# The low half of the converted 64-bit weights subtracted on VectorE instead of on GpSimd

## The chip, the cores and the metric

The kernel runs on one core of a Trainium2 chip. The metric is the device time of one execution in microseconds (us). Five engines work side by side, each through its own list of instructions in order: TensorE (PE; its weight loads are PEld), VectorE (DVE), ScalarE (ACT), GpSimd (POOL), and SyncE (SP), which issues most of the DMAs. A measurement of this kernel can tell a change of about 0.2%, which is 3.0 us.

## The reference

```
# attention: q, k, v are [8, 8, 576, 64]; blocks of 64 tokens, causal by block
scores = q @ k^T / 8, masked where block_i < block_j
attn = exp(scores - max) / (sum + 1e-9);  x = attn @ v        # -> [8, 576, 512]
# mixing of tokens and of channels; U, V, w_ch1, w_ch2 are float64
u = x + (x^T @ U @ V)^T                                       # rank 32
y = u + relu(u @ w_ch1) @ w_ch2                               # 512 -> 2048 -> 512
# gated convolution; w_val, conv_w, w_out are float64
gate = sigmoid(causal conv of y with conv_w, 5 taps per channel)
out = (gate * (y @ w_val)) @ w_out
```

The weights of the last two parts come as float64, which the chip reads as pairs of 32-bit words.

## The kernel before

**Products.** A product keeps more than one rounded factor: each operand is a high half (rounded to the type that PE multiplies) and a low half (what the rounding left), and three matmuls add high x high, high x low and low x high. `hi_act` (L89) makes a high half on ACT; `lo` (L95) subtracts it from the full value on the engine that it is given.

**Conversion of the weights.** `split64` (L136 to L143) turns one raw tile of 128x512 pairs of words into a high and a low half. Its steps, with their engines, are: SP fetches the raw tile; ACT takes the absolute value of the upper words (L118); DVE clamps it (L120), shifts it (L122), puts sign and exponent back (L123) and adds the bits of the lower words (L141), after which the raw tile is no longer needed; ACT rounds to the high half (L89); the low half is a subtraction (L95). There are two raw tiles, so a fetch waits until the L141 of two conversions before is over. The float32 value `wa` has two buffers early and one late. `split64` runs 40 times: 16 times for `w_ch1` (`split_w1`, output `w1hi` and `w1lo`, four DMAs per raw tile), 16 times for `w_ch2` (`split_w2`, output `wo`, which a DMA stores again), and 8 times for `w_val` and `w_out` (`load_wb`, outputs `wvh`, `wvl`, `woh`, `wol`). The first 32 run from the start to about 277 us, the last eight from 1117 to 1161 us.

**Stages.** Until about 128 us PE works on the attention of the first batch and of its mixing. From there until about 1260 us the channel mixing runs in nine groups of 512 tokens, `h` (L833) and `acc` (L885), and the attention of the later batches is laid between its matmuls. After that come `val` (L975) and `out` (L999).

**Attention around the change.** PE writes the scores `pS` (L416); DVE takes the row maxima (L425, L429) and scales them (L427, L430, L432); ACT takes the exponentials (L440), which frees the PSUM bank; PE turns them (`pE`, L456) and multiplies them with the values (`pPV`, L604); ACT copies the product and its sums out (`xt` L605, `lt` L606); POOL normalises `xt` (L624), and DVE adds the mixed tokens (L705). In the channel mixing ACT takes `hh` (L861) and DVE `hl` (L862).

**What sets the order.** PE's instructions stand in the order of the program. The order on DVE, ACT, POOL and SP comes from a scheduler that runs a model of the kernel when it is built, and a helper's engine and cost are part of what it models.

Of the kernel before, what the change touches and what calls it, by code (L numbers as in the profile page):

```python
# [22 lines left out]
def attn_moe_gate_kernel(ctx: ExitStack, tc: tile.TileContext, q, k, v, U, V, w1, w2, wval, convw, wout, out):  # L23
# [59 lines left out]
    def f32(ap):  # L83
        return ap if ap.dtype == F32 else ap.bitcast(F32)

    vec, act, pool, pe, sp = nc.vector, nc.scalar, nc.gpsimd, nc.tensor, nc.sync

    def hi_act(o, i):
        act.copy(o, i)  # L89
# [4 lines left out]
    def lo(eng, o, i, h):  # L94
        eng.tensor_tensor(o, i, f32(h), op=ALU.subtract)  # L95
# [20 lines left out]
    def magnitude(a, h):  # L116

        act.activation(a, f32(h), AF.Abs)  # L118
        with behind(where[0]):
            vec.tensor_scalar(a, a, F64_TINY, None, op0=ALU.max)  # L120
        au = a.bitcast(U32)
        vec.tensor_scalar(au, au, 3, 0x3FFFFFFF, op0=ALU.logical_shift_left, op1=ALU.bitwise_and)  # L122
        vec.scalar_tensor_tensor(au, h, 0xC0000000, au, op0=ALU.bitwise_and, op1=ALU.bitwise_or)  # L123
# [12 lines left out]
    def split64(raw, n, hi_out, lo_out, shape):  # L136

        a = stg["w"].tile([P, GS], F32, tag="wa", name="wa")[:, 0:n]
        au = a.bitcast(U32)
        magnitude(a, raw[:, :, 1])  # L140
        vec.scalar_tensor_tensor(au, raw[:, :, 0], 29, au, op0=ALU.logical_shift_right, op1=ALU.bitwise_or)  # L141
        hi_act(hi_out, shape(a))
        lo(pool, lo_out, shape(a), hi_out)  # L143

    ctx.enter_context(tc.manual_schedule(engines={mybir.EngineType.PE}))
    dram = ctx.enter_context(tc.tile_pool(name="dram", bufs=1, space=DRAM))
# [644 lines left out]
    def split_w1(f):  # L791
        fs = slice(f * P, (f + 1) * P)
        if is64(w1):
            r = stg["raw"].tile([P, GS, 2], U32, tag="raw64", name="raw64")
            hold(r)
            for d in range(ND):
                sp.dma_start(out=r[:, d * P:(d + 1) * P, :], in_=words(w1)[d * P:(d + 1) * P, fs, :])
            split64(r, DM, w1hi[:, :, fs], w1lo[:, :, fs], lambda x: x.rearrange("p (d f) -> p d f", f=P))
            return
        st = fetch(w1, DM, [(slice(0, P), slice(d * P, d * P + P), slice(d * P, d * P + P), fs) for d in range(ND)])  # L800
        st = st.rearrange("p (d f) -> p d f", f=P)
        hi_act(w1hi[:, :, fs], st)
        lo(pool, w1lo[:, :, fs], st, w1hi[:, :, fs])

    def split_w2(f):
        if is64(w2):
            r = stg["raw"].tile([P, GS, 2], U32, tag="raw64", name="raw64")
            hold(r)
            sp.dma_start(out=r, in_=words(w2)[f * P:(f + 1) * P])
            t = stg["o"].tile([P, 2, DM], F32R, tag="wo", name="wo")  # L810
            split64(r, DM, t[:, 0, :], t[:, 1, :], lambda x: x)
        else:
            st = fetch(w2, DM, [(slice(0, P), slice(0, DM), slice(f * P, (f + 1) * P), slice(0, DM))])
            t = stg["o"].tile([P, 2, DM], F32R, tag="wo", name="wo")
            hi_act(t[:, 0, :], st)
            lo(pool, t[:, 1, :], st, t[:, 0, :])
        sp.dma_start(out=w2_s[f], in_=f32(t))
# [85 lines left out]
    def load_wb(b_p):  # L903
        for nm, src in (("v", wval), ("o", wout)):
            h_ = b_p.tile([P, ND, DM], F32R, name=f"w{nm}h")
            l_ = b_p.tile([P, ND, DM], F32R, name=f"w{nm}l")
            wv[nm] = (h_, l_)
            for d in range(ND):
                if is64(src):
                    r = stg["raw"].tile([P, DM, 2], U32, tag="raw64", name="raw64")  # L910
                    sp.dma_start(out=r, in_=words(src)[d * P:(d + 1) * P])
                    split64(r, DM, h_[:, d, :], l_[:, d, :], lambda x: x)
                else:
                    st = stg["raw"].tile([P, DM], F32, tag="raw32", name="raw32")
                    sp.dma_start(out=st, in_=src[d * P:(d + 1) * P, :])
                    hi_act(h_[:, d, :], st)
                    lo(pool, l_[:, d, :], st, h_[:, d, :])
# [245 lines left out]
```

## Time and profile before

| | before |
|---|---|
| median of 3 runs | 1480.73 us (1478.81 to 1481.48) |
| span of the profiled execution | 1473.3 us |
| PE busy | 1426.3 us (97%) |
| DVE busy | 1054.8 us (72%) |
| ACT busy | 718.5 us (49%) |
| POOL busy | 297.8 us (20%) |

The median lies 7.4 us above the span of the one profiled execution; the span counts from the first to the last instruction that the profiler saw. Engines overlap, so the busy shares don't add up. PE idles for 47 us in all, and a part of the program in which PE never stops hides whatever happens on the other engines.

### The profile page before, as it was taken

How to read it: one execution, taken by the hardware profiler on the slowest of the kernel's cores; microseconds unless marked ns; L12 is line 12 of the kernel's file. 1: busy time of each engine (PE TensorE's matmuls, PEld its weight loads, DVE VectorE, ACT ScalarE, POOL GpSimd, SP SyncE). 2: the span in 40 equal slices, each digit the busy share in tenths (PEclk: the TensorE clock that was granted, in tenths of full speed). 3: DMA queues.
4: the chain of work that ended last, by engine and by line, in shares of the span. 5: the costliest groups of instructions: out<-in, count | busy, mean ns of one | idle time of the engine just before them, and what ended most of it. 6: DMA issues, size and time to landing. Idle time of an engine off the chain costs nothing.

```text
span 1473.3 us, 20082 instructions
## 1 busy us (share of the span) xinstructions
PE 1426.3 (97%) x6706; PEld 1102.3 (75%) x6706; DVE 1054.8 (72%) x2224; ACT 718.5 (49%) x1529; POOL 297.8 (20%) x420
## 2 busy tenths in 40 slices
PE   6888899899999999999999999999999999999999
PEld 3656666677777777777777777777888888788887
DVE  7878877967786888777778878777224326399991
ACT  4676564555555546565555555555322221344332
POOL 2113332212121112112211211121122100343310
PEclk9999999999999999999999999999999999999999
DMA  6445764543343434333434433332255433223311
GB/s 123 104 106 154 217 210 130 152 110 96 84 102 110 95 96 111 96 86 82 124 82 111 114 83 96 96 95 70 86 159 167 147 128 123 92 72 101 109 56 65
DMA packets 246288, 163.56 MB, mean 111 GB/s; under 512 B 197669, under 2 KB 212261, under 8 KB 246186
## 3 DMA queue, kind: packets, MB, share of 16 engines
q1 hardware_dynamic: 246186, 162.29, 39.6%
q8 instruction: 53, 0.87, 0.3%
q14 instruction: 49, 0.40, 0.1%
HBM read 134.98 MB, written 27.26 MB: 110 GB/s over the span
## 4 chain that ended last, share of the span: by engine, by line
PE 82%; DVE 10%; DMA 3%; ACT 2%; issue 1%; SPq 1%; POOL 0%; DVEq 0%; ACTq 0%
PE acc L885 25%; PE h L833 25%; PE pPV L604 8%; PE o L999 7%; PE val L975 6%; PE pS L381 6%; DMA raw<-in_moe_w_ch_dram 1%; DVE wa L123 1%; DVE rq L425 1%; PE pG L680 1%; PE acc L878 1%; PE pS L416 1%; DVE wa L141 1%; PE pT L664 1%; DVE wa L120 1%
## 5 line engine op out<-in xcount | busy, mean ns | idle before, releaser
L885 PE MATMUL acc<-hh,w 128*128 128x512 f32 x1152 | 401.0, 402 | 0.0
L885 PEld LDWEIGHTS acc<-hh,w 128*128 128x128 f32 x1152 | 217.1, 188 | 67.6 <-issue 22.5
L833 PE MATMUL h<-uh,w1hi 128*128 128x512 f32 x576 | 238.5, 414 | 2.3 <-ACT lt L606 1.2
L833 PE MATMUL h<-uh,w1lo 128*128 128x512 f32 x576 | 226.4, 393 | 0.0
L885 PE MATMUL acc<-hl,w 128*128 128x512 f32 x576 | 225.9, 392 | 0.0
L833 PE MATMUL h<-ul,w1hi 128*128 128x512 f32 x576 | 225.7, 392 | 0.0
L862 DVE SCALAR_TENSOR_TENSOR hl<-h,hh 128x512 fp32r<-128x512 f32 x144 | 98.5, 684 | 143.2 <-ACT hh L861 142.0
L861 ACT ACTIVATE hh<-h 128x512 fp32r<-128x512 f32 x144 | 85.9, 596 | 173.9 <-PE h L833 167.9
L833 PEld LDWEIGHTS h<-uh,w1hi 128*128 128x128 f32 x576 | 108.6, 189 | 45.7 <-issue 20.4
L95 POOL TENSOR_TENSOR vlo<-vstk,vhi 128x320 fp32r<-128x320 f32 x46 | 43.0, 934 | 455.3 <-ACT vhi L89 389.2
L833 PEld LDWEIGHTS h<-uh,w1lo 128*128 128x128 f32 x576 | 108.4, 188 | 24.2
L885 PEld LDWEIGHTS acc<-hl,w 128*128 128x128 f32 x576 | 108.8, 189 | 19.8 <-issue 0.7
L833 PEld LDWEIGHTS h<-ul,w1hi 128*128 128x128 f32 x576 | 108.7, 189 | 19.6 <-issue 1.3
L957 DVE SCALAR_TENSOR_TENSOR gt<-yb,cw,gt 128x516 f32<-128x516 f32 (+1 forms) x144 | 115.2, 830 | 1.4
L381 PE MATMUL pS<-tq,tk 64*128 64x320 f32 (+4 forms) x576 | 96.7, 429 | 1.5 <-DVE hl L862 0.8
L95 POOL TENSOR_TENSOR yl<-yb,yh 128x512 fp32r<-128x512 f32 (+7 forms) x64 | 66.9, 1078 | 107.4 <-ACT yh L89 107.3
L386 ACT COPY s<-pS 128x320 f32<-128x320 f32 (+2 forms) x128 | 60.2, 497 | 48.7 <-PE pS L381 47.5
L95 POOL TENSOR_TENSOR ul<-xt,uh 128x512 fp32r<-128x512 f32 (+7 forms) x64 | 53.8, 850 | 108.0 <-ACT uh L89 107.9
L536 ACT ACTIVATE s<-s 128x448 f32<-128x448 f32 (+1 forms) x62 | 44.0, 710 | 64.8 <-DVE s L512 64.8
L381 PEld LDWEIGHTS pS<-tq,tk 64*128 64x128 f32 x576 | 43.8, 185 | 37.8 <-issue 22.2
L512 DVE TENSOR_TENSOR s<-s,mb 128x64 f32<-128x64 f32 (+4 forms) x160 | 68.7, 493 | 0.3
L605 ACT COPY xt<-pPV 64x128 f32<-64x128 f32 (+1 forms) x128 | 50.1, 391 | 25.8 <-PE pPV L604 23.9
(169 smaller groups left out, 2758.8 us busy)
## 6 DMA issues: line engine op xcount, KB each, us to landing
w<-w_s SPq DMA_DIRECT2D x144, 512.0 KB, 3.3
rawq<-in_q_dram SPq DMA_DIRECT2D x128, 72.0 KB, 2.8
rawk<-in_k_dram SPq DMA_DIRECT2D x128, 72.0 KB, 3.1
out_dram<-ot SPq DMA_DIRECT2D x35, 256.0 KB, 2.0
vstk<-in_v_dram SPq DMA_DIRECT2D x64, 128.0 KB, 2.7
raw<-in_moe_w_ch_dram SPq DMA_DIRECT2D x64, 128.0 KB, 2.8
raw<-in_moe_w_ch_dram SPq DMA_DIRECT2D x16, 512.0 KB, 3.9
w_s<-wo SPq DMA_DIRECT2D x16, 512.0 KB, 3.3
```

What stands on the lines that cost most here:

```text
L95: eng.tensor_tensor(o, i, f32(h), op=ALU.subtract)
L381: pe.matmul(t[:, o:o + w], tk[me, kslice(j)], tq[me, a0:a1], start=True, stop=True)
L386: act.copy(stt[n][half_of[j]][:, d:d + o], t[:, 0:o])
L512: noted(3, vec.tensor_tensor(sv(n, j), sv(n, j), mb[:, q0[j]:], op=ALU.subtract))
L604: pe.matmul(o_, l_, r_, start=(i == 0), stop=(i == len(todo) - 1))
L833: pe.matmul(ps[:, 0:n], w[:, d, fs], x[:, d, 0:n], start=(d == 0 and i == 0), stop=(d == ND - 1 and i == 2))
L861: act.activation(hh[:, 0:n], ps[:, 0:n], AF.Relu)
L862: latest[0] = vec.scalar_tensor_tensor(hl[:, 0:n], ps[:, 0:n], 0.0, f32(hh[:, 0:n]), op0=ALU.max, op1=ALU.subtract)
L885: pe.matmul(acc[d][:, 0:n], w[:, wi, ds], x[:, 0:n], start=False, stop=(f == NF - 1 and i == 2))
L957: vec.scalar_tensor_tensor(gt[d][:, 0:gw], y[:, d, j:j + gw], cw[:, d, j:j + 1], gt[d][:, 0:gw], op0=ALU.mult, op1=ALU.add)
L975: pe.matmul(ps[:, 0:n], w[:, d, es], x[:, d, 0:n], start=(i == 0), stop=(i == 3 * ND - 1))
L999: pe.matmul(ps[:m, cs], x[:, e, a:a + m], w[:, e, cs], start=(i == 0), stop=(i == 3 * ND - 1))
```

## The change

The low half in `split64` is subtracted by DVE.

```diff
         magnitude(a, raw[:, :, 1])
         vec.scalar_tensor_tensor(au, raw[:, :, 0], 29, au, op0=ALU.logical_shift_right, op1=ALU.bitwise_or)
         hi_act(hi_out, shape(a))
-        lo(pool, lo_out, shape(a), hi_out)
+        lo(vec, lo_out, shape(a), hi_out)
```

PE's list of instructions stays as it was. On the other engines the scheduler gives other orders. In the rows below a name ends with the number of its buffer.

DVE at the place where the second head of a pair is scored, about 137 to 141 us into the profiled execution: `wa_1449` and `wa_1463` are two conversions that follow each other, `pS_1503` is the bank whose maxima lead to L430. Before:

```order
L862 SCALAR_TENSOR_TENSOR hl_1500<-h1_1471,hh_1499 128x512
L425 TENSOR_REDUCE rq_1483<-pS_1503 128x1
L429 TENSOR_TENSOR rq_1483<-rq_1483 128x1
L120 TENSOR_SCALAR wa_1449<-wa_1449 128x512
L430 TENSOR_SCALAR rq_1483<-rq_1483 128x2
L122 TENSOR_SCALAR wa_1449<-wa_1449 128x512
L422 MEMSET pS_1548 64x2x64
L123 SCALAR_TENSOR_TENSOR wa_1449<-raw64_1446,wa_1449 128x512
L425 TENSOR_REDUCE rq_1483<-pS_1548 128x1 x2
L141 SCALAR_TENSOR_TENSOR wa_1449<-raw64_1446,wa_1449 128x512
```

The same place now:

```order
L862 SCALAR_TENSOR_TENSOR hl_1500<-h1_1471,hh_1499 128x512
L420 MEMSET pS_1503 64x64
L141 SCALAR_TENSOR_TENSOR wa_1449<-raw64_1446,wa_1449 128x512
L120 TENSOR_SCALAR wa_1463<-wa_1463 128x512
L425 TENSOR_REDUCE rq_1483<-pS_1503 128x1 x2
L122 TENSOR_SCALAR wa_1463<-wa_1463 128x512
L95 TENSOR_TENSOR wo_1448<-wa_1449,wo_1448 128x512
L429 TENSOR_TENSOR rq_1483<-rq_1483 128x1
L422 MEMSET pS_1548 64x2x64
L123 SCALAR_TENSOR_TENSOR wa_1463<-raw64_1458,wa_1463 128x512
L430 TENSOR_SCALAR rq_1483<-rq_1483 128x2
```

The conversions stand one conversion earlier in DVE's list: before, the scaled maxima L430 stood behind the L120 of `wa_1449`; now they stand behind the L120, L122 and L123 of `wa_1463` and the subtraction of `wa_1449`.

ACT shortly behind that, about 142 to 147 us: `pPV_1597` is the product of PE for tokens 128 to 575 of one head, which L605 and L606 copy out. Before:

```order
L118 ACTIVATE wa_1463<-raw64_1458 128x512
L89 CAST wo_1448<-wa_1449 128x512
L440 ACTIVATE s1_1481<-pS_1548,rq_1483 128x128
L440 ACTIVATE s0_1480<-pS_1548,rq_1483 128x256
L118 ACTIVATE wa_1519<-raw64_1516 128x512
L89 CAST w1hi_148<-wa_1463 128x4x128
L605 COPY xt_1567<-pPV_1597 64x448
L606 COPY lt_1568<-pPV_1597 64x448
```

The same place now:

```order
L89 CAST w1hi_148<-wa_1463 128x4x128
L440 ACTIVATE s1_1481<-pS_1548,rq_1483 128x128
L440 ACTIVATE s0_1480<-pS_1548,rq_1483 128x256
L605 COPY xt_1567<-pPV_1569 64x128
L606 COPY lt_1568<-pPV_1569 64x128
L118 ACTIVATE wa_1533<-raw64_1528 128x512
L89 CAST wo_1518<-wa_1519 128x512
L118 ACTIVATE wa_1650<-raw64_1647 128x512
L605 COPY xt_1567<-pPV_1597 64x448
L606 COPY lt_1568<-pPV_1597 64x448
```

Before, the copies stood behind the absolute value of `wa_1519`; now two more conversions, `wa_1533` and `wa_1650`, have theirs ahead of the copies.

ACT at the same kind of copy one head pair on, about 194 us. Before:

```order
L89 CAST wo_1969<-wa_1970 128x512
L89 CAST w1hi_148<-wa_1984 128x4x128
L118 ACTIVATE wa_2085<-raw64_2082 128x512
L605 COPY xt_1961<-pPV_1999 64x448
L606 COPY lt_1962<-pPV_1999 64x448
```

The same place now:

```order
L89 CAST wo_1969<-wa_1970 128x512
L605 COPY xt_1961<-pPV_1999 64x448
L606 COPY lt_1962<-pPV_1999 64x448
L118 ACTIVATE wa_2085<-raw64_2082 128x512
L89 CAST w1hi_148<-wa_1984 128x4x128
```

Here the copies moved ahead of the absolute value of `wa_2085` and of the rounding of `wa_1984`.

## Rows read from the trace of the kernel before

**Rows 1.** The page, part 1: busy us, share of the span, instructions

```profile
PE 1426.3 (97%) x6706; PEld 1102.3 (75%) x6706; DVE 1054.8 (72%) x2224; ACT 718.5 (49%) x1529; POOL 297.8 (20%) x420
```

**Rows 2.** Windows: from:to, length, busy by engine, granted PE clock, DMA share, GB/s

```profile
120.00:160.00 40.00, 35.82 (x166) 26.04 (x165) 35.30 (x75) 24.93 (x54) 12.77 (x10) 1.00 0.57 167
184.50:187.80 3.30, 3.30 (x9) 2.56 (x10) 3.27 (x8) 3.07 (x8) 1.74 (x2) 0.52 0.71 238
320.00:400.00 80.00, 80.00 (x399) 61.09 (x397) 59.57 (x129) 43.33 (x91) 13.69 (x26) 1.00 0.34 84
1090.00:1170.00 80.00, 80.00 (x356) 66.01 (x355) 30.90 (x53) 22.76 (x41) 19.18 (x17) 1.00 0.58 186
```

**Rows 3.** Timeline of PE: start, us, instruction, [idle before, what ended it]

```profile
49.91 0.66 PE L664 MATMUL pT<-ident,xt 128*128 128x128 f32 x4 [0.79 <-POOL xt L624]
...
86.47 0.33 PE L456 MATMUL pE<-ident,mb 128*128 128x128 f32 x1 [1.53 <-ACT lt L606]
...
91.94 0.66 PE L664 MATMUL pT<-ident,xt 128*128 128x128 f32 x4 [0.91 <-POOL xt L624]
...
108.03 0.30 PE L703 MATMUL pH<-vst,g 128*128 128x64 f32 x1 [1.42 <-DVE xt L705]
...
128.52 0.50 PE L833 MATMUL h<-uh,w1hi 128*128 128x512 f32 x1 [0.99 <-DVE xt L705]
...
139.85 0.49 PE L604 MATMUL pPV<-e,vstk 128*128 128x128 f32 x2
...
147.65 0.33 PE L456 MATMUL pE<-ident,m 128*128 128x128 f32 x1 [0.18 <-ACT lt L606]
...
184.42 0.56 PE L703 MATMUL pH<-vst,g 128*128 128x448 f32 x1 [2.89 <-DVE hl L862]
...
196.72 0.33 PE L456 MATMUL pE<-ident,m 128*128 128x128 f32 x1 [2.41 <-ACT lt L606]
```

**Rows 4.** Line 95 by engine and output: duration ns min/median/max, first and last start

```profile
L95 DVE TENSOR_TENSOR gl<-gf,gh x36: 679/692/1780, 1273.3 to 1449.3; 128x512 fp32r<-128x512 f32 x36
...
L95 POOL TENSOR_TENSOR w1lo<-wa,w1hi x16: 1267/1288/1647, 23.9 to 270.5; 128x512 fp32r<-128x512 f32 x16
```

**Rows 5.** Groups of DVE, 15 to 290 us: busy us, mean ns | idle before

```profile
L123 DVE SCALAR_TENSOR_TENSOR wa<-raw,wa 128x512 uint32<-128x512 uint32 x32 | 28.1, 883 | 0.5
...
L122 DVE TENSOR_SCALAR wa<-wa 128x512 uint32<-128x512 uint32 x32 | 18.9, 596 | 0.5
L120 DVE TENSOR_SCALAR wa<-wa 128x512 f32<-128x512 f32 x32 | 15.6, 494 | 14.6 <-ACT wa L118 14.5
```

**Rows 6.** The same groups of DVE, 1117 to 1162 us

```profile
L123 DVE SCALAR_TENSOR_TENSOR wa<-raw,wa 128x512 uint32<-128x512 uint32 x8 | 5.5, 692 | 0.3
...
L122 DVE TENSOR_SCALAR wa<-wa 128x512 uint32<-128x512 uint32 x8 | 3.4, 428 | 0.3
```

**Rows 7.** Timeline of POOL and DVE around 147 us

```profile
146.70 1.27 POOL L95 TENSOR_TENSOR w1lo<-wa,w1hi 128x512 fp32r<-128x512 f32 x1 [2.01 <-ACT w1hi L89]
...
146.81 1.71 DVE L123 SCALAR_TENSOR_TENSOR wa<-raw,wa 128x512 uint32<-128x512 uint32 x1
```

**Rows 8.** Timeline of ACT, 139 to 195 us

```profile
139.01 0.58 ACT L440 ACTIVATE s<-pS,rq 128x384 f32<-128x384 f32 x1 [1.25 <-DVE rq L430]
...
141.99 0.66 ACT L118 ACTIVATE wa<-raw 128x512 f32<-128x512 f32 x1 [0.73 <-DMA raw<-in_moe_w_ch_dram]
...
153.83 0.66 ACT L118 ACTIVATE wa<-raw 128x512 f32<-128x512 f32 x1 [1.57 <-DMA raw<-in_moe_w_ch_dram]
...
194.91 0.67 ACT L118 ACTIVATE wa<-raw 128x512 f32<-128x512 f32 x1 [0.35 <-DMA raw<-in_moe_w_ch_dram]
```

**Rows 9.** Timeline of DVE, 134 to 183 us

```profile
134.89 1.66 DVE L141 SCALAR_TENSOR_TENSOR wa<-raw,wa 128x512 uint32<-128x512 uint32 x1
...
176.33 1.25 DVE L120 TENSOR_SCALAR wa<-wa 128x512 f32<-128x512 f32 x1
...
182.25 1.28 DVE L123 SCALAR_TENSOR_TENSOR wa<-raw,wa 128x512 uint32<-128x512 uint32 x1
```

## The prediction, made before the changed kernel ran

> **What bounds the kernel now.** I read the busy shares first. PE is busy for 1426.3 of 1473.3 us, so it idles for 47.0 us in all [rows 1]; nothing outside PE's stops can change the time by itself. The windows say where these stops are not: from 320 to 400 us PE is busy for 80.00 of 80 us, and the same in 1090 to 1170 us, where the last eight conversions run [rows 2]. They are early: in 120 to 160 us PE has 35.82 of 40 us, and DVE, with 35.30, is as full [rows 2]. So the 32 early conversions lie where DVE and PE are both near full, the eight late ones where PE hides everything.
>
> The timeline of PE gives the early stops one by one. I took those whose releaser is an engine that the change touches: POOL's normalised `xt` (0.79 and 0.91 us), ACT's copies of `pPV` (1.53, 0.18 and 2.41 us), DVE's L705 (1.42 and 0.99 us) and its `hl` (2.89 us) [rows 3]. The row at 139.85 has no stop, but it needs the bank that the exponentials free, and the order now moves these.
>
> **The change part by part: prices.** One subtraction of 128x512 on DVE takes 0.692 us by the median of the same operation on the gate, against 1.288 us on POOL [rows 4]. So 40 instructions leave POOL, 40 x 1.29 = 51.5 us of its list, and DVE gets 40 x 0.692 = 27.7 us: 32 x 0.692 = 22.1 us before 290 us, and 8 x 0.692 = 5.5 us at 1117 to 1161 us. The last I cost at nothing: DVE is busy for 30.90 of 80 us there while PE never stops [rows 2], and the stage that uses these weights comes later (its first subtraction starts at 1273.3 us [rows 4]). Without that cover it would be 5.5 us.
>
> Against this stands what POOL's subtraction takes from DVE. In the mean, early L123 take 883 ns against 692 late, L122 596 against 428, and L120, an operation of L122's kind and size, 494 against the same 428 [rows 5, 6]: 191 + 168 + 66 = 425 ns per conversion, 32 x 0.425 = 13.6 us. One of them shows why: at 146.81 an L123 lasts 1.71 us, and it ends (148.52) only behind the POOL subtraction that runs from 146.70 to 147.97 [rows 7]. A single DVE instruction is held by up to 1.0 us.
>
> [...]
>
> Net, DVE's list before 290 us grows by 22.1 - 13.6 = 8.5 us. What reaches PE is decided by where the pieces stand in the new order.
>
> **The sum, stop by stop** (shift of PE against before).
> - 49.91: `xt` on POOL is no longer behind a subtraction of 1.29 us, so the stop of 0.79 goes: -0.8. 91.94: likewise, -0.9. 86.47: the copies L605, L606 now stand ahead of exponentials, and I take 1.0 of the 1.53 away [rows 3]; bounds 0 and -1.5.
> - 108.03: one subtraction and one L141, 2 x 0.69 = 1.4 us, now stand ahead of L705, and up to three exponentials, like the one of 0.58 at 139.01 [rows 8], stand ahead of the copies that lead there: +2.9 on the stop of 1.42 [rows 3]; bounds 0 and +2.9. Together with the former +0.2.
> - 128.52: one subtraction more in DVE's run ahead of L705, the stop's releaser: +0.8. PE is now 1.0 late.
> - 139.85: this is the step that decides. The exponentials at 139.01 wait for L430 [rows 8]. In the new list L430 stands behind the L120, L122 and L123 of the next conversion, whose raw tile lands late: before, its absolute value starts at 141.99, waiting for the DMA [rows 8], 5.4 us after the L141 that ends at 134.89 + 1.66 = 136.55 and frees the raw tile [rows 9]. In the new order that L141 stands ahead of the row maxima and ends, by 1.0 late plus L120, L122, the subtraction, L123 and L141 (2.9 us), at about 135.0. Then 135.0 + 5.4 + 0.66 for the absolute value = 141.1, and behind it L120, two maxima, L122, the subtraction, L429 and L123, about 3.3 us: the exponentials start at about 144.5 instead of 139.01. PE's `pPV` comes 5.5 late, that is +4.5 on top of the 1.0. Bounds: +3, if the fetch, no longer beside as many others, takes a third less; +6, if the L141 gains nothing.
> - 147.65: the copies of `pPV` stood behind one absolute value and now stand behind two more. The last of them takes a tile whose predecessor in before started at 153.83, waiting for a DMA [rows 8]; the copies then end at about 155 instead of 147.6, so PE is 7.4 late: +1.9. Bounds 0 and +4.
> - 184.42: three DVE instructions ahead of this stop are held, from 1.25 us at 176.33 to 1.28 at 182.25 [rows 9], together 2.4 us too long; one subtraction comes in: -1.7 of the stop of 2.89. Bounds 0 and -2.4.
> - 196.72: the copies move ahead of an absolute value that starts at 194.91, waiting for a DMA [rows 8]: the stop of 2.41 goes: -2.4. Bounds 0 and -2.4.
> - 200 to 290: 0.27 us more DVE work per conversion against lighter POOL: 0, bounds -2 and +2.
> [...]
>
> Sum: 0.2 + 0.8 + 4.5 + 1.9 - 1.7 - 2.4 + 0 + 1.2 = +4.5. I take 1.0 off, since PE's later stops before 320 us take up part of any delay: +3.5. The profiled span of 1473.3 becomes 1476.8; the median lies 7.4 above the span, so the time is 1480.7 + 3.5 = 1484.2.
>
> [...]
>
> **The rivals.**
> - Faster, because the holds count and the subtractions don't. DVE idles for 14.6 us before its early L120, waiting for the absolute value [rows 5]; a subtraction that falls into such a gap costs nothing, while the holds sit on the way to PE's stops. It would save the two stops on POOL (1.7), 1.0 at 86.47, the holds before 184.42 (1.7 or more) and 2.4 at 196.72, together about 7; if a third is given back at 108.03 and 139.85, -4.2: 1476.5. For it: the held rows. Against it: the subtraction stands behind the L122 of the next conversion, so DVE waits for the tile first and subtracts afterwards. It decides if the stop at 139.85 grows by less than 2 us.
> - No change: the delays and gains fall into the 47 us in which PE idles and cancel: 1480.7. For it: the terms have both signs and nearly the same size. Against it: at 139.85 PE has no idle time to give.
> [...]
> - That the change doesn't do what it says is excluded: all 40 subtractions stand in DVE's list.
>
> **How the numbers follow.** The forecast case has a chance of 0.50, with a range of its own of 1481 to 1489; faster 0.26, no change 0.16, DVE as the bound 0.08. A measurement tells 0.2%, 3.0 us. Of the forecast case 0.17 lies within that of before (its centre is at +3.5), 0.33 above; of the faster case 0.24 is faster by more and 0.02 within; of no change 0.14 is within and 0.02 faster; the last is slower. This gives faster 0.26, same 0.33, slower 0.41. The range reaches from just below the faster case, 1475.5, to just below the last one, 1491.5.
>
> **What would show it.** The groups before 290 us should have L123 near 692, L122 near 428 ns and 32 subtractions near 692 ns on DVE: this shows the prices. A stop of PE of 4 us or more before the `pPV` near 140 us, ended by ACT's exponentials, shows the deciding step; the stops behind `xt` L624 near 50 and 92 us and that behind L606 near 197 us should be gone. PE without a stop from 1090 to 1170 us shows that the late eight cost nothing. I am wrong in the main if the `pPV` near 140 us starts without a stop, or if PE reaches 320 us of the old trace no later than before.

## The result, and the profile after

The changed kernel took 1485.7 us (median of 5 runs, 1482.6 to 1491.4), the kernel before 1480.73 us. The ratio is 1.0056, with a 95% interval of 1.004 to 1.0072: it is slower by about half a percent. The two medians alone differ by 5.0 us, a ratio of 1.0034; why the ratio is larger than that isn't shown here, but the run below with the same order and the old engine gives 1.0055 again. The forecast was 1484.2 us and slower; the loss came out larger than the 3.5 us forecast, and, as the runs below show, only in part at the place that was to decide.

The two profiled executions lie farther apart than the medians: spans of 1473.3 and 1485.9 us, 12.6 us, since the one of before was among the fastest of its kind and the one of after among the slower ones. Places are read from the traces below, sizes from the ratios.

The page of the changed kernel, part 1, answers to [rows 1]:

```profile
PE 1433.4 (96%) x6706; PEld 1105.8 (74%) x6706; DVE 1060.7 (71%) x2264; ACT 718.3 (48%) x1529; POOL 244.4 (16%) x380
```

POOL lost 53.4 us, DVE gained 5.9. PE took 7.1 us more for the same 6706 matmuls, at a mean granted clock of 0.988 instead of 0.994, so part of the difference between the two traces is clock. The windows of after (columns as in [rows 2]; the fourth is a stretch of 4.2 us inside the second) show where:

```profile
80.00:120.00 40.00, 32.96 (x151) 21.70 (x150) 29.26 (x88) 24.56 (x61) 5.85 (x6) 0.91 0.48 120
120.00:160.00 40.00, 30.22 (x122) 21.51 (x122) 32.52 (x75) 23.51 (x53) 3.58 (x3) 0.87 0.52 147
160.00:200.00 40.00, 37.90 (x179) 28.30 (x178) 33.93 (x78) 24.56 (x52) 2.59 (x2) 1.00 0.69 209
145.60:149.80 4.20, 4.20 (x11) 3.38 (x12) 3.04 (x10) 1.18 (x2) 0.00 (x0) 0.50 0.44 129
320.00:400.00 80.00, 79.42 (x392) 61.74 (x391) 61.75 (x139) 42.81 (x91) 12.29 (x22) 1.00 0.41 104
1090.00:1170.00 80.00, 80.00 (x355) 65.88 (x355) 36.52 (x64) 24.50 (x43) 11.87 (x11) 1.00 0.53 172
```

From 120 to 160 us PE is busy for 30.22 us at a mean granted clock of 0.87, where it had 35.82 us at 1.00 [rows 2]. At 1090 to 1170 us, with seven of the eight late subtractions, PE never stops, as before, nor does it up to 1180 us, behind the last. The stops themselves, in the timeline of PE:

```profile
95.10 0.44 PE L456 MATMUL pE<-ident,m 128*128 128x128 f32 x2 [0.68 <-ACT lt L606]
...
96.83 0.33 PE L456 MATMUL pE<-ident,m 128*128 128x128 f32 x1 [1.08 <-DVE x L95]
...
99.51 0.48 PE L456 MATMUL pE<-ident,m 128*128 128x128 f32 x1 [1.58 <-ACT lt L606]
...
111.27 0.33 PE L456 MATMUL pE<-ident,mb 128*128 128x128 f32 x1 [1.80 <-ACT lt L606]
...
133.95 0.50 PE L703 MATMUL pH<-vst,g 128*128 128x512 f32 x2 [1.12 <-DVE g L95]
...
145.41 0.79 PE L833 MATMUL h<-uh,w1hi 128*128 128x512 f32 x1 [4.57 <-ACT s L440]
...
153.29 0.49 PE L604 MATMUL pPV<-e,vstk 128*128 128x128 f32 x2 [1.92 <-ACT mb L440]
...
192.92 0.47 PE L703 MATMUL pH<-vst,g 128*128 128x448 f32 x1 [1.11 <-DVE hl L862]
...
234.71 1.02 PE L381 MATMUL pS<-tq,tk 64*128 64x448 f32 x2 [1.60 <-DVE hl L862]
...
303.96 1.43 PE L381 MATMUL pS<-tq,tk 64*128 64x320 f32 x2 [2.20 <-ACT s L386]
```

The two stops behind POOL's `xt` (0.79 and 0.91 us [rows 3]) are gone but for 0.07 us of the first. A stop of 4.57 us stands near 140 us, ended by the exponentials, and one of 1.92 us at the `pPV`; before, the same matmuls started at 134.00 and 139.85 us without a stop. Before, the matmul of the last row but one had a stop of 0.79 us, and that of the last row none. PE's list is the same in both kernels, so each matmul can be matched with the same one of before: PE is 4.9 us later than before at 115 us of the old trace, 15.0 at 145, 6.6 at 200 and 12.9 at 320; from there on the lateness stays. So all of the difference arises before 320 us, and 6.3 us of it behind 200 us.

The groups of DVE, 15 to 295 us, answer to [rows 5]:

```profile
L123 DVE SCALAR_TENSOR_TENSOR wa<-raw,wa 128x512 uint32<-128x512 uint32 x32 | 21.7, 687 | 0.3
L122 DVE TENSOR_SCALAR wa<-wa 128x512 uint32<-128x512 uint32 x32 | 14.0, 449 | 0.3
L120 DVE TENSOR_SCALAR wa<-wa 128x512 f32<-128x512 f32 x32 | 13.4, 425 | 13.6 <-ACT wa L118 13.5
L95 DVE TENSOR_TENSOR w1lo<-wa,w1hi 128x512 fp32r<-128x512 f32 x16 | 13.1, 819 | 8.3 <-ACT w1hi L89 8.3
L95 DVE TENSOR_TENSOR wo<-wa,wo 128x512 fp32r<-128x512 f32 x16 | 12.4, 778 | 1.1 <-ACT wo L89 0.9
```

The holds of L120, L122 and L123 went, 13.5 us together (62.6 less 49.1), against 13.6 forecast; the 32 subtractions cost 25.5 us, at 798 ns each in the mean instead of 692 (their medians, 691 and 682 ns, are as priced; a few last up to 1.92 us). Why some are longer, and how the place near 140 us comes about, the timeline of all engines shows (the last column is the idle time before, and what ended it):

```profile
137.15 1.27 POOL L95 TENSOR_TENSOR ul<-xt,uh 128x512 fp32r<-128x512 f32 x1 [20.23 <-ACT uh L89]
...
137.27 1.44 DVE L122 TENSOR_SCALAR wa<-wa 128x512 uint32<-128x512 uint32 x1
...
138.38 1.62 POOL L624 TENSOR_TENSOR xt<-xt,t 128x576 f32<-128x576 f32 x1
...
138.63 1.92 DVE L95 TENSOR_TENSOR wo<-wa,wo 128x512 fp32r<-128x512 f32 x1
...
140.58 0.68 ACT L118 ACTIVATE wa<-raw 128x512 f32<-128x512 f32 x1 [2.85 <-DVE wo L95]
...
142.04 0.41 DVE L120 TENSOR_SCALAR wa<-wa 128x512 f32<-128x512 f32 x1
...
142.96 0.41 DVE L122 TENSOR_SCALAR wa<-wa 128x512 uint32<-128x512 uint32 x1
...
144.49 0.14 DVE L427 TENSOR_SCALAR rq<-rq 128x1 f32<-128x1 f32 x1
...
144.66 0.69 ACT L440 ACTIVATE s<-pS,rq 128x512 f32<-128x512 f32 x1 [1.51 <-DVE rq L427]
```

POOL's other work, the `ul` of the mixing and the normalised `xt`, still holds DVE: L122 takes 1.44 us and the new subtraction 1.92. The absolute value of the conversion after next waits for that subtraction, which frees its buffer `wa`; the row maxima and their scaling (L427) stand behind that conversion's L120 and L122 in DVE's list; the exponentials wait for the scaled maxima, and PE for the bank that the exponentials free.

### The profile page after: what moved, and what is told of

Same layout as the page of the kernel before. It is cut to its first block, busy times and chain, and to the rows that moved or that the text cites. A ratio compares the mean times of both kernels' runs of the same rounds, so it can differ in the third digit from the quotient of the medians.

```text
span 1485.9 us, 20083 instructions
## 1 busy us (share of the span) xinstructions
PE 1433.4 (96%) x6706; PEld 1105.8 (74%) x6706; DVE 1060.7 (71%) x2264; ACT 718.3 (48%) x1529; POOL 244.4 (16%) x380
## 4 chain that ended last, share of the span: by engine, by line
PE 84%; DVE 6%; ACT 4%; DMA 3%; issue 1%; SPq 1%; POOL 0%; DVEq 0%; ACTq 0%; POOLq 0%
PE acc L885 26%; PE h L833 25%; PE pPV L604 9%; PE o L999 7%; PE val L975 6%; PE pS L381 6%; DMA raw<-in_moe_w_ch_dram 2%; PE pS L416 2%; PE acc L878 1%; PE pG L680 1%; DVE rq L425 1%; ACT s L440 1%; PE pT L664 1%; DMA rawk<-in_k_dram 1%; PE pE L456 1%
## 5 line engine op out<-in xcount | busy, mean ns | idle before, releaser
L381 PE MATMUL pS<-tq,tk 64*128 64x320 f32 (+4 forms) x576 | 100.6, 434 | 6.6 <-ACT s L386 3.7
L624 POOL TENSOR_TENSOR xt<-xt,t 128x576 f32<-128x576 f32 x32 | 45.7, 1427 | 155.0 <-DVE t L623 139.4
```

Of the source, the lines that this page charges most:

```text
L381: pe.matmul(t[:, o:o + w], tk[me, kslice(j)], tq[me, a0:a1], start=True, stop=True)
```

## The experiments

Two theories stood at the start. A: the loss comes from the places that the scheduler gave the pieces of the conversions. B: it comes from the subtractions' own time on a full DVE. To part them, the order on DVE, ACT and SP was written out as a table and laid on the program by edges that are meant to set the order and make nothing wait. (No run holds the old order with the old engine; that the edges cost nothing rests on the second run, which has them and comes out at 1.0004.) All ratios are against the kernel before on the same chip, with 95% intervals, in five rounds.

**The new order with the old engine.**

```diff
     with _tile.TileContext(nc, schedule_with_timeline_sim=True) as tc:
         attn_moe_gate_kernel(tc, *args)
+        _forced(nc, tc, _mybir)   # the lists of the changed kernel, without its 40 subtractions
```

> GpSimd subtracts, as before, but the instructions on VectorE, ScalarE and SyncE stand in the order that the changed kernel has (the 40 subtractions left out of the list; they stand where the scheduler puts them on GpSimd). Theory A (the loss comes from the places: row maxima, exponentials and copies now stand behind pieces of a conversion that wait for a raw tile): as slow as the changed kernel or slower, since GpSimd's holds of VectorE come on top: 1484 to 1491 us, with a stop of TensorE of 4 us or more near 140 us. Theory B (the loss comes from 22 us of subtractions on a VectorE that is nearly full): no loss, 1478 to 1482 us.

Measured: 1485.29 against 1476.93 us, ratio 1.0055 (1.004 to 1.007). The same loss, with not one subtraction moved. Its trace has the place near 140 us too (timelines of ACT and PE):

```profile
140.62 0.66 ACT L118 ACTIVATE wa<-raw 128x512 f32<-128x512 f32 x1 [5.33 <-POOL wo L95]
...
144.84 0.80 PE L833 MATMUL h<-uh,w1hi 128*128 128x512 f32 x1 [4.08 <-ACT s L440]
...
151.48 0.49 PE L604 MATMUL pPV<-e,vstk 128*128 128x128 f32 x2 [1.42 <-DVE hl L862]
```

Here, too, the absolute value waits for a buffer `wa` that a subtraction frees, on POOL this time, and not for a raw tile.

**The old order with the new engine.**

```diff
-        lo(pool, lo_out, shape(a), hi_out)
+        lo(vec, lo_out, shape(a), hi_out)
...
+        _forced(nc, tc, _mybir)   # the lists of before; the scheduler places only the 40 subtractions
```

> VectorE subtracts, as in the changed kernel, but all other instructions on VectorE, ScalarE and SyncE keep the order that they had before; the scheduler places only the 40 subtractions between them. Theory A: no loss, perhaps a gain, as 13.6 us of holds go and many subtractions fall into gaps of VectorE: 1475 to 1482 us, and no stop over 3 us near 140 us. Theory B: as slow as the changed kernel, 1484 to 1488 us. The L123 should take 0.69 us in the mean in either.

Measured: 1477.59 against 1476.93 us, ratio 1.0004 (0.9993 to 1.0015). Theory A holds in both directions, and B falls: the engine of the 40 subtractions is worth nothing in sum, the order half a percent. The largest stop near 140 us is 1.35 us here. L123 takes 685 ns in the mean, so the holds are gone, and yet the stop that ends at 184.42 us before (2.89 us [rows 3]) doesn't shrink (timeline of PE):

```profile
190.14 0.47 PE L703 MATMUL pH<-vst,g 128*128 128x448 f32 x1 [3.03 <-DVE hl L862]
```

**The eight late subtractions alone.**

```diff
-                    split64(r, DM, h_[:, d, :], l_[:, d, :], lambda x: x)
+                    split64(r, DM, h_[:, d, :], l_[:, d, :], lambda x: x, vec)   # GpSimd for the other 32
```

> Only the eight conversions of w_val and w_out are subtracted by VectorE, the 32 early ones by GpSimd; the order on VectorE and ScalarE is that of before. Both theories: no change, 1480.7 within 2 us, and TensorE never stops from 1090 to 1170 us. If the late eight cost something, up to 5.5 us more.

Measured: 1476.52 against 1476.93 us, ratio 0.9995 (0.9982 to 1.0009). Nothing, as both had it.

**Which part of the order.** The next three runs keep GpSimd and take the new lists in one part only. The cuts lie where old and new list hold the same instructions, at about 113 and 174 us of the profile before (the expectations were written with 122 or 117 and 172 in mind). With cuts at about 122 and 170 us the lists of the middle and of the last part wait for each other, and there is no time of them.

```diff
+        _forced(nc, tc, _mybir)   # new order up to 113 us, the order of before behind that
```

> GpSimd subtracts. Only the front of the lists has the new order, up to about 122 us of the profile (attention of the first batch); behind that stands the order of before. Theory P (the place near 140 us decides, as the prediction has it): 1 to 3 us slower than the kernel before on the same chip. Theory M (many places add up): about 5 us slower, since in the run with the whole new order TensorE was that late at 122 us already, and nothing behind that gives it back.

Measured: 1481.66 against 1476.77 us, ratio 1.0027 (1.0013 to 1.0041). That is 4.0 us by the ratio and 4.9 by the medians, more than P gave and nearer to M.

```diff
+        _forced(nc, tc, _mybir)   # new order from 113 to 174 us
```

> GpSimd subtracts. Only the middle of the lists has the new order, from about 117 to 172 us of the profile, with the place near 140 us; before and behind it the order of before. The front alone cost 0.27% (4 us) by now. Theory P (the place near 140 us decides): 5 to 8 us slower than the kernel before, with a stop of TensorE of 4 us or more near 140 us. Theory M (many places add up, the front the most): 3 to 5 us slower with that stop. If later stops of TensorE take the delay up again (184 and 197 us stand as before): under 2 us in spite of the stop.

Measured: 1481.5 against 1477.28 us, ratio 1.0037 (1.0023 to 1.0052). That is 5.5 us by the ratio and 4.2 by the medians, so this run alone doesn't part the theories; the stop of 4 us or more came as two, of 3.41 and 1.41 us. Its timeline of PE has both stops of the place and, behind them, what gives time back:

```profile
141.34 0.50 PE L833 MATMUL h<-uh,w1hi 128*128 128x512 f32 x1 [3.41 <-ACT s L440]
...
148.06 0.49 PE L604 MATMUL pPV<-e,vstk 128*128 128x128 f32 x2 [1.41 <-DVE hl L862]
...
169.50 0.87 PE L680 MATMUL pG<-x,ust 128*128 128x256 f32 x5 [0.77 <-ACT m L440]
...
186.33 0.47 PE L703 MATMUL pH<-vst,g 128*128 128x448 f32 x1 [1.26 <-DVE hl L862]
...
198.50 0.33 PE L456 MATMUL pE<-ident,m 128*128 128x128 f32 x1 [3.85 <-ACT lt L606]
```

Against before PE falls back by 9.6 us between 115 and 145 us, and is then 4.7 us nearer at 180 and 7.9 at 190: the stops of 2.31 and 2.89 us, which end at 163.67 and 184.42 before, shrink to 0.77 and 1.26 here, with the stretches of lower clock that followed them (120 to 160 us now has a mean granted clock of 0.87, 160 to 200 us 1.00 instead of 0.91). The last row, 3.85 us against 2.41 before, takes part of this away again.

```diff
+        _forced(nc, tc, _mybir)   # new order from 174 us on
```

> GpSimd subtracts. Only the lists from about 172 us on have the new order. The prediction's terms at 184 and 197 us, copies ahead of absolute values, give 2 to 4 us faster than the kernel before, if nothing behind 200 us takes it back; the run with the whole new order was 1 us less late at 320 us than at 160 us, by which this run would be 0 to 2 us faster.

Measured: 1480.39 against 1477.28 us, ratio 1.0019 (1.0005 to 1.0033): slower, where I expected faster. Its timeline shows what became of the term at 197 us (all engines):

```profile
195.59 0.33 PE L456 MATMUL pE<-ident,m 128*128 128x128 f32 x1 [0.28 <-ACT lt L606]
...
196.65 0.67 ACT L118 ACTIVATE wa<-raw 128x512 f32<-128x512 f32 x1 [1.11 <-DMA raw<-in_moe_w_ch_dram]
...
197.86 0.92 ACT L457 COPY e<-pE 128x384 f32<-128x384 f32 x2
...
198.40 0.33 PE L456 MATMUL pE<-ident,m 128*128 128x128 f32 x1 [2.15 <-ACT e L457]
```

The stop of 2.41 us behind the copy L606 [rows 3] shrinks to 0.28, as forecast, but the absolute value that waits for its raw tile now stands ahead of the next copy, L457, and PE stops for 2.15 us a few matmuls later. Nothing is gained. The loss itself stands elsewhere. One stop belongs to the cut: of the matmul that starts at 172.18 us before, where before has 0.57 us and the changed kernel none, and where the last run below, with the same cut, has 1.62 (timeline of PE):

```profile
174.49 0.33 PE L456 MATMUL pE<-ident,mb 128*128 128x128 f32 x1 [2.05 <-ACT lt L606]
```

The others are the two of the changed kernel behind 200 us: 1.69 us at 230.27 and 2.20 at 300.50 here. PE falls back by 5.2 us between 200 and 320 us.

So theory M, many places, holds, and P, one place that decides, falls: the front and the last part cost something of their own, each clear of no change. The traces say the same by place. How far PE falls back against before, in us, in all kept traces, those of the runs further below among them (one execution each; the run with the first seven on GpSimd and the scheduler's own order is left out):

| of the old trace | where this part has the new order | where it has the old one |
|---|---|---|
| 90 to 115 us | 4.6 to 5.1 (4 traces) | 0.0 to 2.0 |
| 115 to 150 us | 8.9 to 9.3 (3 traces) | -1.4 to 1.1 |
| 200 to 320 us | 4.7 to 6.3 (4 traces) | -1.5 to 1.1 |

Between 150 and 200 us the three traces with the new middle give back 4.6 to 7.5 us. The three parts add up to 0.83%, the whole is 0.55% (the first run): with about 0.14% of uncertainty on each of them the difference is suggested, not shown; what PE gives back behind the new middle, and the stop at the cut of the last part, would both make the sum too large.

**The engine by stage.** With the order of before held, the engine was split.

```diff
+        turn[0] += 1
-        lo(pool, lo_out, shape(a), hi_out)
+        lo(pool if turn[0] <= 7 else vec, lo_out, shape(a), hi_out)
...
+        _forced(nc, tc, _mybir)   # the lists of before
```

> The order of before throughout. The first seven conversions (to about 128 us) are subtracted by GpSimd, the other 33 by VectorE; the scheduler places these subtractions. In the run with all 40 on VectorE and the old order, TensorE was 7 us later than before at 115 us and gave 2 us of it back by 320 us. If these are the two halves of the engine's effect (a cost where TensorE waits for VectorE's maxima, a gain where held instructions run free), this kernel is 1 to 3 us faster than the one before; if the 7 us were chance of one execution, there is no difference within 1.5 us.

Measured: 1474.36 against 1477.28 us, ratio 0.9981 (0.9968 to 0.9993). This is faster than both kernels, by little and just clear of no change. The mirror image:

```diff
-        lo(pool if turn[0] <= 7 else vec, lo_out, shape(a), hi_out)
+        lo(vec if turn[0] <= 7 else pool, lo_out, shape(a), hi_out)
```

> The mirror of the run by stage: the order of before throughout, the first seven conversions subtracted by VectorE, the other 33 by GpSimd. All 40 on VectorE in the old order came out at 1.0004, the last 33 alone at 0.9981. If the two stages add up, the first seven alone cost 0.23%: 1.0015 to 1.0031, 2 to 4.5 us slower. If the result by stage was chance, 0.999 to 1.001.

Measured: 1481.33 against 1477.09 us, ratio 1.0033 (1.002 to 1.0046). So the zero of the old order with the new engine is, within the intervals, a sum of two: a loss in the first 128 us and a gain behind. The groups of DVE in the kernel before, first 15 to 128 us and then 128 to 290, show why:

```profile
L123 DVE SCALAR_TENSOR_TENSOR wa<-raw,wa 128x512 uint32<-128x512 uint32 x7 | 4.8, 685 | 0.1
...
L122 DVE TENSOR_SCALAR wa<-wa 128x512 uint32<-128x512 uint32 x8 | 3.3, 416 | 0.1
```

```profile
L123 DVE SCALAR_TENSOR_TENSOR wa<-raw,wa 128x512 uint32<-128x512 uint32 x25 | 23.3, 938 | 0.4
...
L122 DVE TENSOR_SCALAR wa<-wa 128x512 uint32<-128x512 uint32 x24 | 15.6, 656 | 0.4
```

Early the conversions lie far apart, so POOL's subtraction meets no conversion on DVE and holds nothing: moving it only adds work to DVE, and the three `wo` among the moved ones (here in the mirror image, 15 to 128 us) take 1175 ns in the mean: one of them 1.58 us from 48.00 on, beside POOL's `xt` (47.63, for 1.40 us), another 0.68 us at 80.29, where POOL does nothing:

```profile
L95 DVE TENSOR_TENSOR wo<-wa,wo 128x512 fp32r<-128x512 f32 x3 | 3.5, 1175 | 0.0
```

That this work reaches PE by way of the row maxima and the copies behind them is argued, not shown; what the trace has is that PE's stops at 86.47 and 108.03 us of before, 1.53 and 1.42 us [rows 3], are 2.02 and 1.80 in the mirror image. Later one conversion follows the other, and POOL's subtraction of one meets L122 and L123 of the next. In the run by stage the later groups fall to:

```profile
L123 DVE SCALAR_TENSOR_TENSOR wa<-raw,wa 128x512 uint32<-128x512 uint32 x25 | 16.9, 685 | 0.5 <-DVE r L619 0.2
...
L122 DVE TENSOR_SCALAR wa<-wa 128x512 uint32<-128x512 uint32 x24 | 11.1, 470 | 0.3
```

**The same split, with the scheduler's own order.** The edit of the run by stage without the written order.

> The first seven conversions on GpSimd, the other 33 on VectorE, and the scheduler orders all engines as it likes (its lists are those of before up to about 130 us, and its own behind that). If the engine alone made the gain of the run by stage, 0.997 to 0.999 again. If the order behind 130 us is worth as much as the runs with the new middle (1.0037) and the new last part (1.0019) say, the result is open between 0.998 and 1.005; with the maxima at the place near 140 us no longer behind the next conversion, as its list shows, I expect no slower than 1.001.

Measured: 1481.41 against 1477.09 us, ratio 1.0021 (1.0005 to 1.0038). My expectation of no more than 1.001 failed. The place near 140 us has only a stop of 1.77 us, but others have grown (timeline of PE):

```profile
143.62 0.49 PE L607 MATMUL pPV<-e,vstk 128*128 128x128 f32 x2 [1.77 <-ACT mb L443]
...
167.46 1.44 PE L683 MATMUL pG<-x,ust 128*128 128x256 f32 x5 [3.75 <-ACT m L443]
...
188.94 0.47 PE L706 MATMUL pH<-vst,g 128*128 128x448 f32 x1 [3.02 <-DVE rq L432]
...
200.06 0.33 PE L459 MATMUL pE<-ident,m 128*128 128x128 f32 x1 [2.84 <-ACT lt L609]
```

(Lines are 3 higher there.) The same engines for the same subtractions, in two orders, differ by 0.4%.

**The changed kernel with the old middle.** VectorE subtracts all 40; the lists are those of the changed kernel, except from 113 to 174 us.

```diff
+        _forced(nc, tc, _mybir)   # new order, the order of before from 113 to 174 us
```

> The changed kernel (VectorE subtracts all 40, new order) with only the middle of the lists, 117 to 172 us, in the order of before. If the place near 140 us carries the loss of the changed kernel (1.0056), most of it goes: 1.001 to 1.003. If the parts only partly add up, since a later stop takes up what an earlier one delays, less than half of it goes: 1.003 to 1.0055.

Measured: 1482.53 against 1477.09 us, ratio 1.0028 (1.0014 to 1.0042). About half of the loss goes with the middle, half stays. The value lies in the range given for the place near 140 us as the carrier of the loss, but the interval reaches far into the other one, so this run alone doesn't part the two.

## Why the prediction was right, and where it was wrong

- **Direction and cause: right.** The sum rested on where the new order puts the pieces, not on 22 us of subtractions, and the first two experiments show just that. The size was short: +3.5 us against a ratio that stands for about 8 us (0.56%), or 5.0 us between the medians. That 1484.2 lies 1.5 us from the measured 1485.7 is in part luck: two stretches that the sum had at +0.2 and 0 cost 4.9 and 6.3 us in the trace, and PE gave back 7.5 us between 150 and 200 us, more than the terms there.
- **Prices: right but for one.** The holds gave back 13.5 us, and the late eight cost nothing. The subtraction was priced at 0.69 us by a median, and its medians are that; the mean is 0.80, since some are held beside POOL's other work (1.92 us at 138.63), which the price left out.
- **The mean over the stretch: wrong.** "425 ns per conversion" was a mean from 15 to 290 us. The holds all lie behind 128 us; in front of it there are none, and there the change cost 0.33% by the engine alone.
- **The step "up to 108.03, together +0.2": wrong.** The front of the order costs 0.27%. The +2.9 at 108.03 didn't come: that stop went, and 1.80 us stands at the copies ahead of it (111.27 in the new trace). I worked through the stops that the trace of before has, and the new ones stand elsewhere: at 95 to 100 us of after there are three (0.68, 1.08 and 1.58 us), where before went through, since there, too, scaled maxima and copies came to stand behind a conversion that waits for its raw tile. It is the mechanism that the sum had for the place near 140 us, some 45 us earlier. The timeline of ACT of the changed kernel has it: the absolute value waits 2.80 us for its raw tile, and the exponentials of the next maxima start at 97.15, after 2.10 us of idle time, where they started at 93.85 before.

```profile
93.31 0.67 ACT L118 ACTIVATE wa<-raw 128x512 f32<-128x512 f32 x1 [2.80 <-DMA raw<-in_moe_w_ch_dram]
...
97.15 0.58 ACT L440 ACTIVATE s<-pS,rq 128x384 f32<-128x384 f32 x1 [2.10 <-DVE rq L430]
```

- **The step at 128.52, +0.8: right in sum.** A new stop of 1.12 us (133.95 in the new trace) stands just ahead of it, and PE is 0.8 us later behind both.
- **The step at 139.85 "that decides": the order right, the wait behind it another, the place one exponential earlier, the share too large.** The forecast had 5.5 us at the `pPV`, ended by the exponentials behind L430. The trace has 4.57 us one step earlier, at an `h` that waits for the exponentials behind L427, and 1.92 at the `pPV`. Maxima did come to stand behind the next conversion, but what made it late was a buffer `wa` that a subtraction freed late (140.58 above, and 140.62 in the first run), not the landing of its raw tile, from which the sum worked the 5.5 us out. PE fell back by 10 us between 115 and 145 us, but the middle alone costs 0.37%, since later stops take part of it up: the 1.0 us taken off for this was too little.
- **The step at 147.65, +1.9: wrong.** The stop of 0.18 us goes: PE comes there 14.7 us later than before and doesn't wait for the copies.
- **The step at 184.42, -1.7: right in size, not in its reason.** The stop is 1.11 us instead of 2.89. The reason given was that DVE's holds go; but without the holds and in the old order it stays, 3.03 us in the second run, and with POOL's subtractions and the new order it is 1.00 in the first. The order shrinks it.
- **The step at 196.72, -2.4: the stop shrank as forecast, to 0.28 us, the gain did not come.** I did not ask what stands behind the copies in the new list; the wait moved to L457, where PE now stops for 1.71 us.
- **The step "200 to 290: 0, bounds -2 and +2": wrong, and the largest miss by place.** PE falls back by 6.3 us between 200 and 320 us, and by 4.7 to 6.3 in every trace with the new lists there. The term weighed DVE's added work and followed no list there. Of the two new stops of this stretch, 1.60 and 2.20 us, neither was in the sum; with the stretches of lower clock behind them (0.50 from 237 to 239 and from 303.9 to 308 us) they are where PE loses the time. The last part of the order costs 0.19% on its own.
- **Clock.** The sum has +1.2 us for it, and no run shows that term. What the traces show is the granted clock behind single stops. In the changed kernel it is 0.50 behind those near 100, 112, 145 and 153 us (100 to 102, 114 to 116, 145.6 to 149.8 and 155 to 157 us) and behind the two past 200 us (237 to 239 and 303.9 to 308 us). Before, it was 0.53 behind the stop at 163.67 (164 to 167 us) and 0.52 behind the one at 184.42 [rows 2]; both stretches are gone, since 160 to 200 us has 1.00 now instead of 0.91. PE needs 7.1 us more for the same matmuls. How much of this is the kernel's isn't shown: PE is busy for 1433.0 us in the second run, too, which loses nothing.
- **The rival "faster, because the holds count"** was half right: with the order held, the 33 later subtractions gain 0.19%, and the first seven eat it. Its own sum has a slip: a third of 7 us given back leaves 4.7, not 4.2, and 1476.0, not 1476.5.
- **DVE as the bound.** No run shows this case, nor the 1491.5 at the end of the range that goes with it: with all 40 subtractions on DVE and the old order the second run has a ratio of 1.0004.

## What to carry to other kernels

Where a scheduler orders the engines, moving one operation to another engine changes two things, the work and every list; hold the lists fixed in one run and the engine in another before explaining either. Price an engine's contention stage by stage: a mean over the program can hide a stage that pays and one that gains, and the split of the two can beat both kernels. And for each stop that a new order removes, read which instruction stands next behind the piece that waits: a wait for a transfer or a buffer that stays in an in-order list only changes whom it holds (in the run with the new last part L606, 0.28 us left of 2.41, and then L457, 2.15 us). List the terms that a sum puts at nothing, too: here the largest miss was one of them.

## What the runs showed of the hardware that I had not expected

DVE's L122, which reads one tensor, is held as L123 is, which reads two (1.71 us at 146.81 [rows 7]): 1.44 us beside POOL's subtraction `ul` (137.27 above), 0.43 in the mean of the late conversions before [rows 6]. The prediction had counted this hold in its means, without a reason. And taking the conversions' subtractions off POOL did not end the contention: what POOL still does in this stage held the moved subtraction itself, up to 1.92 us against a median of 0.68.
